# Rows of the spectral remap written four partitions apart instead of next to each other

## The chip, the cores and the metric

The kernel runs on one core of one Trainium2 chip. The metric is the device time of one execution in microseconds (us). A core has five engines that run side by side and wait for each other through semaphores: TensorE (PE; its weight loads are listed apart as PEld), VectorE (DVE), ScalarE (ACT), GpSimd (POOL) and SyncE (SP). SP issues nearly all of this kernel's DMAs; 16 DMA engines carry them out. SBUF, the on-chip memory, has 128 rows (partitions); PSUM takes TensorE's results.

## The reference

One input `x` of 2048 tokens by 448 channels goes through two branches, and a gate mixes them.

```python
S, D = 2048, 448
g = sigmoid((x * gate_w).sum(-1, keepdims=True))
# a: softmax attention, 16 heads of 28
q, k, v = split(x @ wqkv)                      # per head
a = merge(softmax(q @ k.T * 28 ** -0.5) @ v) @ wo
# b: a filter in the frequency domain
X = rfft2(x, axes=(tokens, channels))          # 2048 x 225, complex
b = irfft2(X * (w_r + 1j * w_i)).astype(bfloat16)
out = g * a + (1 - g) * b
```

Inputs and output are bfloat16. This text is about branch b and about what attention waits for while b is computed.

## The kernel before

**Attention is the frame.** The 16 heads are taken in four groups of four (`g`), the queries in four blocks of 512 (`c`): 16 stages of attention. In each, TensorE multiplies keys by queries into PSUM (`psA`, three heads' tiles at a time, and `psB`, two), ScalarE takes the exponential of the whole tile into a ring in SBUF (L1093, `ring<-psA`, `ring<-psB`), and TensorE multiplies the result with the values (`pvb`). A share of the exponentials is made on VectorE instead (L1051 and L1061, `y` and `pd`). At the end of a stage `normalise` turns the sums around: a DMA moves the sums out of `pvs` (`rs<-pvs`, L1192), VectorE takes the reciprocal (L1195) and splits it (`rhl`, L1196 and L1197), two DMAs bring the parts into eight rows (`r<-rhl`), and TensorE spreads them over the rows (`bg<-r,cst`), after which VectorE scales the stage's output (L1206).

**The spectral branch is background work.** `background` computes the two-dimensional transform as matrix products that fill TensorE's time between the attention's matmuls. First the channels are transformed (`X1`, one tile of 450 = 2 x 225 values per 128 tokens, 16 tiles). The 2048 tokens are then split as 2048 = 16 x 128, in two steps. `stage_a` multiplies each of the 16 tiles by a matrix of 128 points (three matmuls, `bg<-X,R`), VectorE copies the result from PSUM into one of three buffers `Y` (L1385), and a DMA remaps it into `U` (L1387): the 128 rows of `Y`, numbered 16 j + g with j from 0 to 7 and g from 0 to 15, become 8 rows of `U` with 16 pieces of 450 values each. After all 16 tiles, `U[:, g, :]` has in its 128 rows 16 tiles t times 8 values of j, and one matrix product per g with the table `CS` finishes the transform (`bg<-U,CR`). VectorE multiplies by the filter `w_r + i w_i` (L1427 to L1443) back into `X1`, and the inverse goes the same way: `stage_a` again with 16 remaps, then products with the table `RB` (L1465 to L1468, `bg<-CR,U`), then the inverse over the channels. Each remap moves 128 pieces of 900 bytes, 112.5 KB; there are 16 of them forward and 16 in the inverse. The first product that reads `U` waits for all 16.

**What sets the order.** A list scheduler (`Sched`) places every operation by due times and estimated costs while the program is built; each engine's order is then fixed, and each engine works strictly in that order. All DMAs named here stand in one queue, SP's. The scheduler counts a remap as 0.62 us of SP and 2.0 us until it has landed. Waits between engines come from the tiles that are written and read; a `Y` buffer is written again only when the remap that reads it has landed.

The line of the change is L1387. `rows_of(ap, row0, stride, count, dims)` (L37) names `count` rows from `row0` on, `stride` rows apart; `J` is 8, `NT` is 16, `F2` is 450. The tables `CS` and `RB` are made on the host in `fft_consts` and have their rows in the order of `U`'s rows.

## Time and profile before

| what | value |
|---|---|
| median of 3 runs | 441.5 us (441.43 to 446.78) |
| the profiled execution: its time | 443.47 us |
| its span, first to last instruction | 441.7 us |
| mean granted TensorE clock | 0.965 |
| instructions | 8904 |
| remaps `U<-Y` | 32 of 112.5 KB, 98.1 to 278.3 us, 0.61 us of SP each |
| attention's small DMAs | 15 `rs<-pvs` of 8 KB, 30 `r<-rhl` of 4 KB |
| all DMA packets | 25,902, 16.64 MB |

The profile is a record of one execution. Busy time says how long an engine was at work; a row of the timeline has the start and length of an instruction, the engine and line, what it writes and reads, and in brackets how long the engine had been idle before it and what ended that. The windows view gives busy time per engine for a stretch of the span, with the number of instructions, and then the granted TensorE clock (1.00 is full speed), the DMA engines' busy share and GB/s. The chain of waits goes back from the last instruction to what released it, step by step; its DMA pieces run from the issue to the landing. The digits of a row such as `PEclk` are tenths, one for each fortieth of the span.

### The profile page before, as it was taken

The page shows a single profiled execution, that of the slowest core. Times are in us where ns is not written, and L with a number is a line of the kernel's source. Part 1 is how long each engine was busy: PE and PEld are TensorE (multiplying, and loading weights), DVE is VectorE, ACT ScalarE, POOL GpSimd, SP SyncE. Part 2 cuts the span into 40 slices and gives each one's busy share as a digit, 9 for nine tenths or more (in the row PEclk, how much of TensorE's full clock was granted, in tenths as well). Part 3 has the DMA queues.
Part 4 walks back from the last instruction along what each step waited for, and adds up shares of the span by engine and source line. Part 5 has one row for each costly group of instructions (what it writes and reads, how often), then busy time and mean ns, then how long its engine had stood idle before and what let it go on. Part 6 is the DMA issues. An engine that isn't in the chain of part 4 may idle for free.

```text
span 441.7 us, 8904 instructions
## 1 busy us (share of the span) xinstructions
PE 405.2 (92%) x3498; PEld 145.1 (33%) x3498; DVE 341.8 (77%) x643; ACT 408.8 (93%) x379; POOL 35.3 (8%) x72
## 2 busy tenths in 40 slices
PE   8999999998998989998999959799999998999997
PEld 5443332232442232223433312212344332332233
DVE  6555678676679899998689756676877889799964
ACT  3999999998999999998999958868999999999992
POOL 3404001000022000000040000000003000000000
PEclk9999999999999999997999988957999999999999
DMA  8400100013413120110011442200001010010101
GB/s 228 113 1 3 28 11 1 2 45 70 87 42 58 39 59 22 43 40 4 2 39 32 54 50 44 47 2 24 11 25 38 14 49 3 12 34 10 36 22 62
DMA packets 25902, 16.64 MB, mean 38 GB/s; under 512 B 10456, under 2 KB 24580, under 8 KB 25860
## 3 DMA queue, kind: packets, MB, share of 16 engines
q1 hardware_dynamic: 25092, 15.82, 16.0%
q8 instruction: 27, 0.44, 0.4%
q10 hardware_dynamic: 768, 0.25, 0.3%
q14 instruction: 15, 0.12, 0.1%
HBM read 10.19 MB, written 1.84 MB: 27 GB/s over the span
## 4 chain that ended last, share of the span: by engine, by line
ACT 50%; PE 25%; issue 12%; DVE 7%; DMA 6%; ACTq 0%; DVEq 0%
ACT ring L1093 49%; PE bg L527 9%; PE pvb L527 6%; PE psA L527 5%; PE psB L527 4%; DMA rs<-pvs 2%; DMA U<-Y 2%; DVE y L1051 1%; DVE Y L1385 1%; DMA r<-rhl 1%; DMA U<-in_A_wqkv_dram 1%; DVE pd L1061 1%; PE bg L530 1%; ACT w L899 0%; DVE k L837 0%
## 5 line engine op out<-in xcount | busy, mean ns | idle before, releaser
L1093 ACT ACTIVATE ring<-psA 128x1536 bf16<-128x1536 f32 x177 | 287.9, 1626 | 12.2 <-PE psA L527 11.0
L1093 ACT ACTIVATE ring<-psB 128x1024 bf16<-128x1024 f32 x177 | 211.9, 1197 | 6.4 <-PE bg L527 3.4
L1051 DVE TENSOR_SCALAR y<-bg 128x512 uint16<-128x512 f32 x140 | 94.5, 685 | 34.2 <-PE bg L527 33.2
L1061 DVE TENSOR_SCALAR pd<-y 128x2048 uint16<-128x2048 uint16 x140 | 94.3, 691 | 1.1 <-PE pvb L527 0.6
L527 PEld LDWEIGHTS <-k 32*128 32x128 bf16 x1024 | 46.9, 91 | 132.3 <-issue 124.6
L527 PE MATMUL psA<-q,k 32*128 32x512 bf16 x531 | 72.3, 393 | 17.0 <-ACT ring L1093 13.8
L527 PE MATMUL pvb<-ring,vw 128*32 128x512 bf16 x884 | 83.0, 395 | 0.0
L527 PE MATMUL psB<-q,k 32*128 32x512 bf16 x353 | 72.4, 393 | 1.5 <-ACT ring L1093 1.3
L527 PE MATMUL pvb<-pd,vd 128*32 128x512 bf16 x560 | 57.6, 401 | 0.0
L527 PE MATMUL bg<-q,k 32*128 32x512 bf16 x140 | 53.0, 395 | 0.2 <-DVE y L1051 0.2
L527 PEld LDWEIGHTS <-vw 128*32 128x32 bf16 x884 | 20.3, 95 | 29.0 <-issue 25.9
L527 PEld LDWEIGHTS <-xT 128*128 128x128 bf16 x320 | 19.2, 99 | 19.2 <-issue 17.8
L904 POOL CAST vw<-w 128x16 bf16<-128x16 f32 x16 | 4.4, 283 | 259.3 <-ACT w L899 259.3
L527 PE MATMUL bg<-X,R 128*128 128x225 bf16 (+1 forms) x96 | 19.3, 301 | 5.0 <-DVE k L837 2.5
L1385 DVE CAST Y<-bg 128x450 bf16<-128x450 f32 x32 | 19.5, 621 | 3.5 <-PE bg L527 2.5
L960 POOL TENSOR_SCALAR vd<-vf 128x348 bf16<-128x348 f32 x16 | 19.8, 1236 | 14.5 <-DVE vf L949 6.3
L527 PEld LDWEIGHTS <-vd 128*32 128x32 bf16 x560 | 14.8, 95 | 15.7 <-issue 14.1
L527 PE MATMUL bg<-xT,wpq 128*128 128x512 bf16 (+1 forms) x60 | 18.8, 390 | 0.1
L527 PE MATMUL bg<-xT,wpk 128*128 128x512 bf16 (+1 forms) x60 | 17.9, 383 | 0.3 <-DVE xT L803 0.3
L527 PE MATMUL bg<-Bd,ZT 113*128 113x448 bf16 x64 | 18.0, 370 | 0.1
L527 PE MATMUL bg<-Bd,xT 128*128 128x450 bf16 x64 | 17.9, 359 | 0.1
L1355 DVE CAST X<-bg 128x450 bf16<-128x450 f32 x16 | 10.0, 623 | 9.0 <-PE bg L527 9.0
(114 smaller groups left out, 346.7 us busy)
## 6 DMA issues: line engine op xcount, KB each, us to landing
U<-Y SPq DMA_DIRECT2D x32, 112.5 KB
CR<-cRB SPq DMA_DIRECT2D x8, 256.0 KB
xtok<-in_A_x_dram SPq DMA_DIRECT2D x4, 448.0 KB
out_dram<-fin SPq DMA_DIRECT2D x14, 112.0 KB
CR<-cCS SPq DMA_DIRECT2D x8, 192.0 KB
Wg<-in_B_w_r_dram SPq DMA_DIRECT2D x8, 112.5 KB
Wg<-in_B_w_i_dram SPq DMA_DIRECT2D x8, 112.5 KB
U<-in_A_wqkv_dram SPq DMA_DIRECT2D x2, 252.0 KB
```

Source lines behind the costliest of these rows:

```text
L527: self.pin(self.nc.tensor.matmul(out, lhsT=lhsT, rhs=rhs, start=start, stop=stop, **kw))
L530: self.pin(self.nc.tensor.transpose(out=out, in_=in_, identity=self.c("ident")[0:n, 0:n]))
L904: self.pin(nc.gpsimd.tensor_copy(out=free_dims(self.vw[g][:], [[128, 4], [32, 4]], 4 * b * 128 + DH), in_=self.w[g][:, 4 * b:4 * b + 4, :]))
L960: self.pin(nc.gpsimd.tensor_scalar(out=self.vd[:, f, :, :, 0:DH + 1], in0=self.vf[:], scalar1=PHGAIN[f], scalar2=None, op0=ALU.mult))
L1051: self.pin(nc.vector.tensor_scalar(out=ys[:, s, :], in0=self.bgi(it), scalar1=127 * UNITS, scalar2=0.0, op0=ALU.add, op1=ALU.max))
L1061: self.pin(nc.vector.tensor_scalar(out=fl(pds).bitcast(U16), in0=fl(ys), scalar1=float(PHASE[f]), scalar2=0.25, op0=ALU.add, op1=ALU.mult))
L1093: self.pin(nc.scalar.activation(out=self.ring[:, u0:u0 + len(st), :], in_=slot[:, 0:len(st), :], func=ACT.Exp, scale=LN2 / UNITS))
L1355: self.pin(nc.vector.tensor_copy(out=self.X1[:, t, :], in_=self.bgi(it)[:, 0:F2]))
L1385: self.pin(nc.vector.tensor_copy(out=y[:], in_=self.bgi(it)[:, 0:F2]))
```

## The change

The 8 rows into which a remap writes are no longer next to each other. For tile t and row j the row in `U` was 8 t + j; it becomes `spread(t, j)` = 32 (t // 4) + 4 j + t % 4. So tile 0 wrote rows 0 to 7 and now writes rows 0, 4, 8, ... 28; tile 1 wrote rows 8 to 15 and now writes 1, 5, ... 29; tiles 4 to 7 fill rows 32 to 63, and so on. All 128 rows are still filled once. The rows of the tables `CS` and `RB` are permuted in the same way on the host, so that the products with `U` add up the same terms. The columns of the tables, and with them everything behind the products, stay. Each engine executes the same instructions in the same order with the same waits as before.

```diff
+def spread(t, j):
+    return 32 * (t // 4) + 4 * j + t % 4
...
-            CS[g, j::J, 0, j::J] = np.cos(th)
-            CS[g, j::J, 1, j::J] = np.sin(th)
-            CS[g, j::J, 2, j::J] = -np.sin(th)
+            rows = [spread(t, j) for t in range(NT)]
+            CS[g, rows, 0, j::J] = np.cos(th)
+            CS[g, rows, 1, j::J] = np.sin(th)
+            CS[g, rows, 2, j::J] = -np.sin(th)
...
-            RB[g2, j2::J, 0, j2:P:J] = np.cos(ps)
-            RB[g2, j2::J, 0, P + j2::J] = np.sin(ps)
...
+            rows = [spread(t, j2) for t in range(NT)]
+            RB[g2, rows, 0, j2:P:J] = np.cos(ps)
+            RB[g2, rows, 0, P + j2::J] = np.sin(ps)
...
-                d = self.dma(rows_of(self.U[:], t * J, 1, J, [[F2, NT], [1, F2]]), y[:], [e] + war, k, dur=0.62, lat=2.0)
+                d = self.dma(rows_of(self.U[:], spread(t, 0), 4, J, [[F2, NT], [1, F2]]), y[:], [e] + war, k, dur=0.62, lat=2.0)
```

More of the change, by code (lines that the diff above doesn't have):

```diff
@@ L73, in fft_consts @@
             ps = 2 * np.pi * (tt * aa / NT + tt * bh / S)
-            RB[g2, j2::J, 0, j2:P:J] = np.cos(ps)
-            RB[g2, j2::J, 0, P + j2::J] = np.sin(ps)
-            RB[g2, j2::J, 1, j2:P:J] = -np.sin(ps)
-            RB[g2, j2::J, 1, P + j2::J] = np.cos(ps)
+            rows = [spread(t, j2) for t in range(NT)]
+            RB[g2, rows, 0, j2:P:J] = np.cos(ps)
+            RB[g2, rows, 0, P + j2::J] = np.sin(ps)
+            RB[g2, rows, 1, j2:P:J] = -np.sin(ps)
+            RB[g2, rows, 1, P + j2::J] = np.cos(ps)
     c["RB"] = RB.reshape(NT // 2, 2, P, 4 * P).transpose(0, 2, 1, 3)
```

## The prediction

> **What bounds the kernel now.** I read the page first: its busy shares, clock row, chain and the DMA that the change touches.

> ```profile
> PE 405.2 (92%) x3498; PEld 145.1 (33%) x3498; DVE 341.8 (77%) x643; ACT 408.8 (93%) x379; POOL 35.3 (8%) x72
> PEclk9999999999999999997999988957999999999999
> ACT 50%; PE 25%; issue 12%; DVE 7%; DMA 6%; ACTq 0%; DVEq 0%
> U<-Y SPq DMA_DIRECT2D x32, 112.5 KB
> ```

> ScalarE's exponentials (L1093) carry half of the chain; DMA carries 6%. The span of 441.7 us cannot shrink below ScalarE's 408.8 us of work plus its head and tail, so what can be won is ScalarE's idle time. The table by stages says where that lies (PE, PEld, DVE, ACT, POOL busy, then clock, DMA share, GB/s):

> ```profile
> 104.50:146.00 41.50, 36.80 (x385) 14.51 (x378) 30.18 (x61) 39.08 (x40) 6.24 (x9) 1.00 0.34 62
> 146.00:204.00 58.00, 53.05 (x453) 16.95 (x451) 57.69 (x122) 58.00 (x54) 0.00 (x0) 1.00 0.15 39
> 204.00:212.00 8.00, 8.00 (x67) 3.12 (x66) 4.67 (x10) 6.63 (x8) 1.05 (x3) 0.58 0.03 4
> 255.00:304.00 49.00, 41.99 (x268) 10.56 (x268) 31.63 (x58) 35.80 (x31) 0.00 (x0) 0.76 0.23 37
> 304.00:430.00 126.00, 118.64 (x1109) 42.34 (x1107) 106.01 (x185) 126.00 (x117) 5.77 (x9) 1.00 0.08 22
> ```

> ScalarE idles 2.42 us in 104.5 to 146, 1.37 us in 204 to 212 and 13.20 us in 255 to 304, and not at all in the two long stages between and after. The first stretch is the forward remap (U<-Y, L1387) and the third holds the inverse remap and what follows. The chain of waits in order of time (start, length in us, what) shows which DMAs stand there:

> ```profile
> 102.62 3.99 DMA rs<-pvs
> 131.90 5.03 DMA U<-Y
> 140.14 4.03 DMA U<-Y
> 249.61 5.44 DMA rs<-pvs
> 258.48 4.46 DMA r<-rhl
> ```

> A U<-Y takes 4 to 5 us from issue to landing, and small transfers beside it also take 4 to 5.4 us. The timeline has one rs<-pvs (8 KB) without company, issued at 125.85 and read by VectorE at 127.75:

> ```profile
> 125.85 0.58 SPq L509 DMA_DIRECT2D rs<-pvs  x1
> 127.75 0.25 DVE L1195 RECIPROCAL rr<-rs 128x16 f32<-128x16 f32 x1 [0.76 <-DMA rs<-pvs]
> ```

> So a small transfer alone is 1.90 us; the ones in the chain are late by 2.1 to 3.5 us because they queue behind U<-Y. Nearly alone, the U<-Y of 140.14 takes 4.03 - 1.90 = 2.13 us more than the small one: 115,200 bytes in 2.13 us, 54 GB/s. Where do these 2.1 us go? The DMA view of the window 140.14 to 144.24 (40 slices of 0.10 us):

> ```profile
> GB/s 53 18 53 0 9 0 0 0 0 0 0 0 88 79 53 88 132 202 184 167 88 35 9 0 0 0 0 0 0 0 0 0 0 0 0 0 0 0 0 0
> ```

> The packets are taken up between slices 12 and 22, 1.2 to 2.3 us after the issue, at up to 202 GB/s. The landing comes 1.7 us after the last of them. The issue and the reading of Y are therefore not the long part; the write side drains for much longer than the packets are taken up.

> **The change part by part.** The two constant tables get their rows permuted on the host: no instruction, no byte more. The row in L1387 becomes four apart. Each engine's instructions, their order and their semaphores stay the same, the DMA still writes 8 rows of 16 pieces of 900 bytes, and SP still issues it in the time it did (a stride between rows is in rs<-pvs already, 0.58 us above). So the only thing with a price is how fast the 8 rows drain.

> The row for it is the 2.13 us above. [...]

> Bounds of the landing after the change, from rows: not below 1.90 us (the 8 KB transfer), and at the upper end 4.03 us (unchanged) or more (rival D). Between them stands the reading of Y, which stays as it is: packets are taken up until 2.3 us after the issue. How soon a landing follows the last packet when nothing drains is seen at the lone rs<-pvs (the window 125.85 to 127.85, slices of 0.05 us):

> ```profile
> GB/s 0 0 0 0 0 0 0 0 0 0 0 0 0 0 0 0 0 0 0 0 0 0 0 0 3 26 32 31 31 31 12 0 0 0 0 0 0 0 0 0
> ```

> Its last packets are in slice 30, at 1.55 us, and it is read at 1.90 us: 0.35 us. So I take 2.3 + 0.4 = 2.7 us. If one row accepted no more than twice today's rate, it would be 1.90 + 1.07 = 3.0 us. A U<-Y in a queue then costs those behind it about 1.1 us, the time in which its packets are taken up, instead of 2.1 us.

> Now each place, with what waited (timeline; the bracket is the idle time before the instruction and its releaser):

> ```profile
> 106.63 0.25 DVE L1195 RECIPROCAL rr<-rs 128x16 f32<-128x16 f32 x1 [2.25 <-DMA rs<-pvs]
> 108.83 1.02 ACT L1093 ACTIVATE ring<-psB 128x1024 bf16<-128x1024 f32 x1 [0.78 <-PE psB L527]
> 110.52 1.45 ACT L1093 ACTIVATE ring<-psA 128x1536 bf16<-128x1536 f32 x1 [0.66 <-PE psA L527]
> 137.03 0.63 DVE L1385 CAST Y<-bg 128x450 bf16<-128x450 f32 x1 [0.65 <-DMA U<-Y]
> 138.49 1.45 ACT L1093 ACTIVATE ring<-psA 128x1536 bf16<-128x1536 f32 x1 [0.42 <-PE psA L527]
> 144.22 0.36 PE L527 MATMUL bg<-U,CR 128*128 128x450 bf16 x1 [0.97 <-DMA U<-Y]
> 145.01 1.02 ACT L1093 ACTIVATE ring<-psB 128x1024 bf16<-128x1024 f32 x1 [0.55 <-PE bg L527]
> 248.20 1.31 SPq L509 DMA_DIRECT2D U<-Y  x2
> 255.08 0.25 DVE L1195 RECIPROCAL rr<-rs 128x16 f32<-128x16 f32 x1 [3.44 <-DMA rs<-pvs]
> 257.55 1.02 ACT L1093 ACTIVATE ring<-psB 128x1024 bf16<-128x1024 f32 x1 [1.70 <-PE psB L527]
> 258.91 1.45 ACT L1093 ACTIVATE ring<-psA 128x1536 bf16<-128x1536 f32 x1 [0.34 <-PE psA L527]
> 263.07 0.58 PE L527 MATMUL bg<-r,cst 8*128 8x512 bf16 x1 [2.76 <-DMA r<-rhl]
> 264.18 1.45 ACT L1093 ACTIVATE ring<-psA 128x1536 bf16<-128x1536 f32 x1 [2.91 <-PE psA L527]
> 278.31 0.63 SPq L509 DMA_DIRECT2D U<-Y  x1
> 284.44 0.62 PE L527 MATMUL bg<-CR,U 128*113 128x256 bf16 x4 [1.95 <-DMA rs<-pvs]
> 285.70 1.45 ACT L1093 ACTIVATE ring<-psA 128x1536 bf16<-128x1536 f32 x1 [1.73 <-PE psA L527]
> ```

> (1) At 106.6 VectorE stands 2.25 us on rs<-pvs, TensorE on VectorE, ScalarE on TensorE for 0.78 + 0.66 us. One U<-Y is ahead of that rs<-pvs; with it 1 to 2 us shorter VectorE's wait is nearly gone: 1.44 us won on ScalarE. (2) At 137.0 a Y buffer is written again only when its transfer of 131.90 has landed; at 2.7 us that is 134.6, before VectorE comes: 0.42 us. (3) At 144.2 the last forward transfer holds TensorE 0.97 us; landing 1.3 us earlier, it doesn't: 0.55 us. (4) At 255.1 rs<-pvs waits behind two U<-Y. It landed 3.5 us later than one alone; about 2 x 1 us of that goes, and since the two ahead no longer pile up (two in 1.31 us, so 0.7 us apart), up to 3 us. VectorE's 3.44 us fall to about 0.5 us and ScalarE wins 1.70 + 0.34 = 2.04 us. (5) At 263.1 r<-rhl behind a U<-Y holds TensorE 2.76 us: landing in 2.2 us instead of 4.46 leaves some 0.4 us, and ScalarE wins 2.5 of 2.91 us. (6) At 284.4 the first inverse matmul on U waits 1.95 us. The row names rs<-pvs, but that was issued 1 us before and takes 1.90; the matmul reads U, so it is the last U<-Y, issued at 278.31 behind another and out for some 6 us. At 3 us it lands at 281.3, before TensorE is free at 284.44 - 1.95 = 282.49: 1.73 us. Sum: 1.44 + 0.42 + 0.55 + 2.04 + 2.5 + 1.73 = 8.7 us.

> That leaves ScalarE's other idle time in 255 to 304: 13.20 - (2.04 + 2.91 + 1.73) = 6.5 us. It lies under a halved TensorE clock (windows; the clock is the third number from the end):

> ```profile
> 104.92:108.33 3.41, 2.11 (x23) 0.70 (x19) 1.59 (x5) 3.13 (x4) 0.25 (x1) 1.00 0.75 121
> 258.52:261.94 3.42, 1.79 (x10) 0.40 (x6) 2.08 (x4) 2.42 (x3) 0.00 (x0) 1.00 0.48 72
> 261.94:268.77 6.83, 5.70 (x34) 1.17 (x34) 2.34 (x4) 3.82 (x3) 0.00 (x0) 0.50 0.47 57
> 282.42:285.83 3.41, 1.46 (x12) 0.69 (x10) 1.64 (x4) 1.68 (x3) 0.00 (x0) 1.00 0.07 6
> 285.83:302.90 17.07, 17.07 (x95) 3.31 (x97) 10.52 (x21) 11.73 (x10) 0.00 (x0) 0.50 0.07 17
> ```

> Each halved stretch follows 3.4 us in which TensorE was busy for only 1.79 (52%) or 1.46 us (43%), and those are exactly the windows that hold waits (5) and (6). The window at 104.92, 62% busy, was followed by no halving. Without the waits the two windows fill to the 91 to 94% of the long stages, so I expect both stretches to go, and with them about 6.4 us. The halving at 204 to 212 (1.37 us) is in a stretch with hardly any DMA (share 0.03) and stays. For what becomes late next (TensorE has 94% in the stage 304 to 430, VectorE 99% in 146 to 204) I keep back 1.5 us. Gain: 8.7 + 6.4 - 1.5 = 13.6 us. The profiled execution took 443.5 us (441.7 us span and 1.8 us around it); 443.5 - 13.6 = 429.9 us. That execution is 2.0 us above the median of the runs, 441.5 us, so the forecast is 441.5 - 13.6, rounded to 428 us.

> **Rivals.** (A) The forecast, 428 us, with its own range from 424 (all of ScalarE's idle time in the three stages gone: 441.5 - 2.42 - 1.37 - 13.20 = 424.5) to 432 (half of the 6.4 us stays, and 1 us more of the waits).

> (B) The waits go, but the clock still halves near the remap. For it: the halved stretch at 204 needs no DMA, and single runs of the kernel lie 5.3 us apart (441.43, 446.78), just what ScalarE loses in the long stretch (17.07 - 11.73 us). Against it: the two stretches follow windows emptier than the one at 104.92. Then 441.5 - 8.7 + 1 = 434 us. [...]

> (C) The change doesn't do what it says: it doesn't matter which rows lie together; the drain is limited by the 8 rows themselves, or by the engines that write them, and stays 2.1 us. Rows: each row takes 14,400 B in 2.13 us, 6.8 GB/s, and no row here shows a single row taking more in a long transfer. Against it: packets are taken up at up to 202 GB/s, so the engines can read that fast. Nothing else changes: 441.5 us. [...]

> (D) Slower: consecutive transfers get into each other's way. Today each U<-Y fills the 8 rows next to those of the one before; afterwards four in a row interleave in the same 32 rows, and so share what those rows share. If two drains could overlap today and can't then, each transfer that queues behind a U<-Y is a drain later, 2.1 us at the four places (1), (4), (5) and (6): 441.5 + 8.4 = 450 us. It decides if the drain stays at 2.1 us and today's transfers do overlap. Against it: the rs<-pvs of 249.61, behind two U<-Y issued 0.7 us apart, is 3.54 us late, and two drains end to end minus these 0.7 us are 2 x 2.13 - 0.7 = 3.56 us. There is no overlap to lose.

> **How the numbers follow.** A 0.60, B 0.22, C 0.13, D 0.05. The range 424 to 438 us holds A and B with their ends, and B with only half of the 8.7 us, which a landing of 3.0 us or more could leave. What a measurement tells from no change is about 2%, 8.8 us: faster means below 432.7 us. Nearly all of A (0.58) and a third of B (0.07) lie there: 0.65. Slower than 450.3 us: about half of D, 0.02. The rest of A, B and D, and C, is within 2%: 0.33.

> **What would show it.** A U<-Y nearly alone at 2.5 to 3.3 us in the chain (right), or still near 4 us (C). rs<-pvs and r<-rhl next to it at 2 to 2.7 us, and VectorE's waits on rs<-pvs, 2.25 and 3.44 us, below 0.7 us. ScalarE's idle time in what was 255 to 304 below 4 us, with a clock row without its 5 and 8 there; if the clock stays halved there with the waits gone, B. The forecast fails if ScalarE, once free of these waits, waits just as long for something that was hidden behind them.

## The result

The changed kernel is faster: 424.85 us in the median of four runs (423.76 to 430.27) against 441.87 us before (441.43 to 446.78); the ratio is 0.958, with a 95% interval from 0.949 to 0.967. The ratio leaves out the run of 430.27 us, which lies more than 1.5% above the fastest. On the 441.5 us that the prediction started from that is 423.0 us, 18.5 us less. Forecast were 13.5 us less, 428 us, and a range from 424 to 438: right in sign and in the places that were won, too small in size, and 1 us past the lower end of the range. The profiled execution took 423.90 us with a span of 422.1 us, 19.6 us shorter than the span before.

The page of the changed kernel, with the rows that were shown of the one before:

```profile
PE 392.4 (93%) x3498; PEld 144.7 (34%) x3498; DVE 341.4 (81%) x643; ACT 406.1 (96%) x379; POOL 35.2 (8%) x72
PEclk9999999999999999999999999999999999999999
ACT 68%; PE 15%; issue 13%; DVE 2%; DMA 1%; ACTq 0%
```

The clock row has no gap any more, DMA fell from 6% of the chain to 1%, and what is left of that belongs to the loads at the start. ScalarE's share of the chain went from 50% to 68%. The table by stages, at the places of the prediction's table (the places (4) to (6), between 255 and 285 us before, now lie 8 to 14 us earlier):

```profile
104.50:146.00 41.50, 39.80 (x409) 15.84 (x408) 33.35 (x70) 41.50 (x42) 6.25 (x9) 1.00 0.25 67
204.00:212.00 8.00, 7.14 (x80) 3.01 (x72) 6.54 (x13) 8.00 (x10) 0.39 (x2) 1.00 0.02 1
255.00:290.00 35.00, 32.96 (x280) 10.69 (x279) 28.85 (x52) 35.00 (x32) 0.00 (x0) 1.00 0.13 35
```

ScalarE is busy for the whole of each: 41.50 of 41.50, 8.00 of 8.00, 35.00 of 35.00. The instructions that waited at the places (1), (3), (4), (5) and (6), in the timeline:

```profile
104.76 0.25 DVE L1201 RECIPROCAL rr<-rs 128x16 f32<-128x16 f32 x1 [0.25 <-DMA rs<-pvs]
141.06 0.36 PE L533 MATMUL bg<-U,CR 128*128 128x450 bf16 x1
247.29 0.25 DVE L1201 RECIPROCAL rr<-rs 128x16 f32<-128x16 f32 x1 [0.32 <-DMA rs<-pvs]
253.44 0.39 PE L533 MATMUL bg<-r,cst 8*128 8x512 bf16 x1
270.89 0.54 PE L533 MATMUL bg<-CR,U 128*113 128x256 bf16 x3
```

VectorE's 2.25 and 3.44 us became 0.25 and 0.32 us. TensorE's 0.97, 2.76 and 1.95 us are gone, and no copy into `Y` waits for a transfer any more (place 2). (The line numbers shown are 6 higher than before.)

### The profile page after: what moved, and what is told of

Its sections match the earlier page's. It is cut to its first block, busy times and chain, and to the rows that moved or that the text cites. A ratio compares the mean times of both kernels' runs of the same rounds, so it can differ in the third digit from the quotient of the medians.

```text
span 422.1 us, 8904 instructions
## 1 busy us (share of the span) xinstructions
PE 392.4 (93%) x3498; PEld 144.7 (34%) x3498; DVE 341.4 (81%) x643; ACT 406.1 (96%) x379; POOL 35.2 (8%) x72
## 4 chain that ended last, share of the span: by engine, by line
ACT 68%; PE 15%; issue 13%; DVE 2%; DMA 1%; ACTq 0%
ACT ring L1099 67%; PE bg L533 6%; PE psA L533 4%; PE pvb L533 3%; PE psB L533 2%; ACT w L905 1%; DMA wv<-in_A_wqkv_dram 1%; PE bg L536 1%; DMA cst<-ccst 1%; DVE y L1057 0%; DVE vw L947 0%; DVE k L688 0%; DVE xtok L1492 0%; DVE q L701 0%; DVE fin L1297 0%
## 5 line engine op out<-in xcount | busy, mean ns | idle before, releaser
L1099 ACT ACTIVATE ring<-psA 128x1536 bf16<-128x1536 f32 x177 | 296.5, 1675 | 1.6 <-PE psA L533 1.6
L1099 ACT ACTIVATE ring<-psB 128x1024 bf16<-128x1024 f32 x177 | 220.7, 1247 | 0.0
L533 PEld LDWEIGHTS <-k 32*128 32x128 bf16 x1024 | 48.8, 91 | 130.8 <-issue 122.0
L533 PE MATMUL psA<-q,k 32*128 32x512 bf16 x531 | 69.7, 381 | 19.9 <-ACT ring L1099 16.1
L533 PE MATMUL pvb<-ring,vw 128*32 128x512 bf16 x884 | 80.7, 384 | 0.0
L533 PE MATMUL psB<-q,k 32*128 32x512 bf16 x353 | 70.1, 382 | 2.1 <-ACT ring L1099 1.8
L533 PE MATMUL pvb<-pd,vd 128*32 128x512 bf16 x560 | 55.2, 384 | 0.0
L533 PE MATMUL bg<-q,k 32*128 32x512 bf16 x140 | 51.1, 383 | 0.2 <-DVE y L1057 0.2
L533 PEld LDWEIGHTS <-vw 128*32 128x32 bf16 x884 | 20.1, 94 | 26.1 <-issue 22.8
L1391 DVE CAST Y<-bg 128x450 bf16<-128x450 f32 x32 | 19.6, 621 | 3.5 <-PE bg L533 3.4
## 6 DMA issues: line engine op xcount, KB each, us to landing
U<-Y SPq DMA_DIRECT2D x32, 112.5 KB
Wg<-in_B_w_r_dram SPq DMA_DIRECT2D x8, 112.5 KB
Wg<-in_B_w_i_dram SPq DMA_DIRECT2D x8, 112.5 KB
```

The costliest lines, as they stand in the source:

```text
L533: self.pin(self.nc.tensor.matmul(out, lhsT=lhsT, rhs=rhs, start=start, stop=stop, **kw))
L1099: self.pin(nc.scalar.activation(out=self.ring[:, u0:u0 + len(st), :], in_=slot[:, 0:len(st), :], func=ACT.Exp, scale=LN2 / UNITS))
L1391: self.pin(nc.vector.tensor_copy(out=y[:], in_=self.bgi(it)[:, 0:F2]))
```

## Experiments

**What the drain depends on.** A kernel of its own sends the remap's 112.5 KB into rows that lie differently, one transfer at a time. It leaves out the computation.

```diff
+    for name, stride in (("Uone", 1), ("Utwo", 2), ("Ufour", 4), ("Ueight", 8), ("Usixteen", 16), ("Utwelve", 12),
+                         ("Vone", 1), ("Vfour", 4), ("Vthirtytwo", 32)):    # U: 8 rows of 16 pieces, V: 4 rows of 32
+        nc.sync.dma_start(out=rows_of(T[name][:], 0, stride, P // n, [[F2, n], [1, F2]]), in_=y[:])
+        nc.vector.tensor_copy(out=y[:, 0:16], in_=T[name][:, 0, 0:16])
...
+    for name, stride in (("Uone", 1), ("Ufour", 4)):     # a small transfer right behind
+        move(name, 0, stride); small(); read_small(); read(name)
+    for name, stride, second in (("Uone", 1, 8), ("Ufour", 4, 1)):     # two in a row
+        move(name, 0, stride); move(name, second, stride); read(name)
```

VectorE's timeline; the bracket is its wait for the transfer. In the first nine rows, one per pattern, SP issues the transfer 0.02 to 0.03 us after the wait begins. Then come the small transfer behind a U transfer with adjacent rows and with rows four apart, and two U transfers in a row. (The first row is from the second of three rounds, the others from the first.)

```profile
106.92 0.17 DVE L54 COPY Y<-Uone 128x16 bf16<-128x16 bf16 x1 [3.91 <-DMA Uone<-Y]
57.94 0.17 DVE L54 COPY Y<-Utwo 128x16 bf16<-128x16 bf16 x1 [3.08 <-DMA Utwo<-Y]
60.77 0.17 DVE L54 COPY Y<-Ufour 128x16 bf16<-128x16 bf16 x1 [2.65 <-DMA Ufour<-Y]
63.99 0.17 DVE L54 COPY Y<-Ueight 128x16 bf16<-128x16 bf16 x1 [3.05 <-DMA Ueight<-Y]
67.23 0.17 DVE L54 COPY Y<-Usixteen 128x16 bf16<-128x16 bf16 x1 [3.06 <-DMA Usixteen<-Y]
70.07 0.17 DVE L54 COPY Y<-Utwelve 128x16 bf16<-128x16 bf16 x1 [2.67 <-DMA Utwelve<-Y]
76.41 0.17 DVE L54 COPY Y<-Vone 128x16 bf16<-128x16 bf16 x1 [6.17 <-DMA Vone<-Y]
79.85 0.17 DVE L54 COPY Y<-Vfour 128x16 bf16<-128x16 bf16 x1 [3.26 <-DMA Vfour<-Y]
84.18 0.17 DVE L54 COPY Y<-Vthirtytwo 128x16 bf16<-128x16 bf16 x1 [4.16 <-DMA Vthirtytwo<-Y]
88.46 0.18 DVE L60 COPY pvs<-rs 128x16 f32<-128x16 f32 x1 [4.11 <-DMA rs<-pvs]
91.99 0.17 DVE L60 COPY pvs<-rs 128x16 f32<-128x16 f32 x1 [3.07 <-DMA rs<-pvs]
98.51 0.17 DVE L54 COPY Y<-Uone 128x16 bf16<-128x16 bf16 x1 [6.06 <-DMA Uone<-Y]
```

All nine waits shown lie within 0.2 us of theory P, in which four neighbouring rows share one way in: four neighbouring rows need 6.17 us, eight (two ways) 3.91 us, rows 2, 8 and 16 apart (four ways) 3.05 to 3.08 us, rows 4 and 12 apart (eight ways) 2.65 and 2.67 us, and four rows 32 apart 4.16 us, which is two ways. The rounds agree within 0.1 us, but for the four rows four apart (3.3 to 3.7 us) and 32 apart (4.2 to 4.3 us). Rows 8 and 16 apart are slower (3.0 us) than rows 4 and 12 apart (2.6 us) although they are spread wider, and four rows 32 apart (4.1 us) cost as much as eight next to each other (3.9 us): nearness alone (Q) and a fixed limit per row (R) are both out as what makes the old order slow. One way for all 112.5 KB takes 6.1 us; less the 1.9 us of a small transfer alone, which was measured in the whole kernels, 4.2 us are left, by this estimate 27 GB/s. The small transfer issued some 0.7 us after a U transfer is read 3.40 us after its own issue behind adjacent rows and 2.32 us behind rows four apart (alone 1.9 us): the queueing is real, and it shrinks, though the 1.5 us behind adjacent rows are less than the 2 us that P had. Two transfers in the old order end 5.9 to 6.0 us after the first issue, so they drain one after the other although their rows are in different groups; the overlap that rival D would have lost does not exist. In the new order, with both in the same ways, VectorE can read 3.7 to 3.8 us after the first issue. With eight ways the next limit shows. The trace closes each U transfer with eight packets of 4 bytes (a remap of the changed kernel, at 137.86 us, too: 128 packets of 900 bytes and eight of 4) and each V transfer with four, from which I take it that eight and four DMA engines write them, one row each. With four ways, eight rows (2 apart) need 3.1 us and four rows (4 apart) 3.3 to 3.7 us; with eight ways eight rows need 2.6 us, about 0.7 us for the 14,400 B of one row, an estimate of some 21 GB/s. Whether it is the engine or the row that takes no more, the probe can't tell.

**A third row order.** The remapped rows 16 apart, with tables to match:

```diff
 def spread(t, j):
-    return 32 * (t // 4) + 4 * j + t % 4
+    return 16 * j + t
```

> Rows 16 apart (16 j + t) in place of four apart, tables permuted to match; all else as in the changed kernel. P: four ways, a remap lands in 2.9 us instead of 2.5; VectorE's and TensorE's waits on the DMAs stay below about 1 us and the time is that of the changed kernel within 1%, 424 to 428 us. Q: 2.5 us and the same time. If any added 0.4 us of landing were exposed at the six places, 424 + 2.4 = 426 us.

425.74 us in the median (425.05 to 430.06), ratio 0.963 (0.956 to 0.970): within 1% of the changed kernel. One wait on a transfer by TensorE came back, 0.54 us on `r<-rhl`, where the changed kernel has none:

```profile
254.78 0.37 PE L533 MATMUL bg<-r,cst 8*128 8x512 bf16 x1 [0.54 <-DMA r<-rhl]
```

So most of the gain is there once a remap lands in 3.0 us instead of 3.9 (the probe's figures for rows 16 and 1 apart); the last 0.4 us of the landing, down to the 2.6 us of rows four apart, are worth little.

**One half of the change at a time.** Forward remaps alone:

```diff
-                d = self.dma(rows_of(self.U[:], spread(t, 0), 4, J, ...
+                d = self.dma(rows_of(self.U[:], spread(t, 0) if inv == 0 else t * J, 4 if inv == 0 else 1, J, ...
```

> Forward remaps write rows four apart, the 16 inverse remaps neighbouring rows as before (the table CS permuted, RB not). Theory T: ScalarE's idle time comes from the waits, place by place, and the halved clock behind 255 us from the waits there. Then the 2.4 us of 104 to 146 are won and nothing of the 13 us after 255: 438 to 440 us, with VectorE waiting 3 us on rs<-pvs and TensorE 2 to 3 us on r<-rhl and U, and one or two halved stretches right behind them. Rival H: the halving is chance and independent of the waits; then halved stretches are as likely elsewhere, and the time lies between 432 and 440 us from run to run.

439.36 us in the median (433.43 to 442.68), ratio 0.984 (0.974 to 0.995), which rests on the runs of 433.43 and 438.59 us. The waits after 250 us are those of the kernel before, one of them shorter (1.49 us for 2.76):

```profile
252.44 0.25 DVE L1201 RECIPROCAL rr<-rs 128x16 f32<-128x16 f32 x1 [3.37 <-DMA rs<-pvs]
260.47 0.40 PE L533 MATMUL bg<-r,cst 8*128 8x512 bf16 x1 [1.49 <-DMA r<-rhl]
283.45 0.62 PE L533 MATMUL bg<-CR,U 128*113 128x256 bf16 x4 [1.95 <-DMA rs<-pvs]
```

The clock was halved from 253.9 to 257.3, from 260.7 to 270.9 and from 284.6 to 294.8 us, behind each of the three, and once more from 199.2 to 206.1. The spread of the run times would nearly suit H as well; that the stretches stand where T has them is what speaks for T.

The inverse remaps alone, by the same edit with the two cases exchanged:

> The other half alone: forward remaps write neighbouring rows as before, the inverse ones rows four apart. T: the 2.4 us of 104 to 146 stay lost, the 13 us after 255 are won with about 2 us of slower restarts: 426 to 428 us, no halved stretch behind 255 us. Together the two halves' gains, about 3 and 14 us, should add up to the 17 us of the whole change. H: a halved stretch in this kernel as often as in the one before.

431.22 us (430.02 to 433.15), ratio 0.974 (0.968 to 0.980). The place, the waits and the clock after 255 us came as T had it:

```profile
255.00:290.00 35.00, 32.59 (x268) 10.70 (x268) 28.99 (x55) 35.00 (x32) 0.00 (x0) 1.00 0.18 45
```

ScalarE is busy throughout, at the full clock. But the time is 3 to 5 us above the expectation, because the clock was halved at two places which have no transfer wait, 159.6 to 166.4 and 204.0 to 210.8 us, and all four runs had 10 to 21 us of halved clock. There H has a point. By the ratios the two halves gain 1.6% and 2.6%, together the whole change's 4.2%, but the first has an interval from 0.5 to 2.6%. By the medians they gain 3.7 and 11.9 us, together 15.6 us against 17.0 us for the whole change: about additive, no closer than that.

**Is it the empty TensorE that halves the clock?** The kernel before, with matmuls of zeros at the waits (5) and (6):

```diff
+            if n == 8:
+                for _ in range(22):
+                    self.mm(self.bgi(it)[:, 0:256], self.zero[:, 0:P], self.zero[:], True, True)
             self.mm(self.bgi(it), self.c("sel8", 8), r8[:], True, True)
...
+                        if g == 0 and fb == 0 and ri == 0:
+                            for _ in range(15):
+                                self.mm(self.bgi(it)[:, 0:256], self.zero[:, 0:P], self.zero[:], True, True)
```

> The kernel before, with neighbouring rows, and 22 matmuls of zeros (256 columns, 0.107 us each, 2.4 us) just ahead of the spread of the sums in stage 8, at the wait (5), and 15 (1.6 us) just ahead of the first inverse product, at the wait (6). They run while TensorE would stand there; their result is overwritten. No transfer is any faster. Theory T: an emptier TensorE in those 3.4 us is what halves the clock; the waits of VectorE and ScalarE stay, the halved stretches behind 262 and 286 us go, and with them 5 to 6 us: 436 to 438 us, with 7 to 10 us of halved clock instead of 27 to 41. Rival H: the halving comes from something else there (the phase of the run, or the total load): as many halved us as before, 441 to 446 us, plus up to 1 us for fillers that are late.

437.54 us (433.78 to 439.36) against 442.99 us, ratio 0.986 (0.977 to 0.996). At (6) the fillers occupy the wait, ScalarE still idles 1.40 us at the next exponential (1.73 before), as its timeline shows:

```profile
284.70 1.81 PE L527 MATMUL bg<-zero 128*128 128x256 bf16 x15
287.65 1.45 ACT L1093 ACTIVATE ring<-psA 128x1536 bf16<-128x1536 f32 x1 [1.40 <-PE psA L527]
```

The table by stages of the same run has the clock (the 1.00 before the last two columns) whole behind it:

```profile
286.38:303.00 16.62, 15.84 (x137) 5.02 (x135) 14.84 (x28) 15.35 (x14) 0.00 (x0) 1.00 0.08 19
```

With no transfer faster, 3.5 to 20.1 us of halved clock remained per run; 7 to 10 us were expected. In the kernel before, on the same chip, it was 17.5 to 41.0 us (one run, whose record says 121 us at an ordinary time, is left out). At (5) a halved stretch stayed, from 258.3 to 265.1 us, right behind wait (4), which had no fillers; those for (5) ran only from 264.6 us on, so they test nothing. At (6) the transfers and ScalarE's wait stayed and only TensorE's emptiness went, and the halving went with it. That rests on one profile with fillers against two without (before, forward alone), and on the halved time of four runs, whose highest (20.1 us) lies above the lowest before (17.5 us).

**Halved time against time.** Each run's halved time follows from its mean clock and span, as (1 - clock) x 2 x span:

| kernel | us of halved clock: time of the run in us |
|---|---|
| before (five of twenty) | 17.5: 438.96; 27.2: 440.70; 30.8: 442.11; 34.5: 444.72; 41.0: 447.66 |
| changed | 0: 423.76; 0: 423.90; 6.8: 425.80; 20.6: 430.27 |
| forward alone | 10.4: 433.43; 23.6: 438.59; 30.7: 440.13; 37.9: 442.68 |
| inverse alone | 11.1: 430.02; 10.3: 431.20; 13.7: 431.25; 20.7: 433.15 |

Within each kernel a halved us goes with about 0.3 us more (0.33 for a straight line through all twenty runs of the kernel before, 0.31 for the changed one). It is most of what the runs of one kernel differ by, not all: seven more of the runs before had 27 us of it, and they lie between 440.07 and 443.18 us. Carried to no halving at all, beyond any run, that line puts the kernel before at about 433 us, some 9 us above the changed one; by this estimate these 9 us are waits. The other 7 to 8 us are halved time, some 30 us less some 7 of it at 0.3.

**Is ScalarE now the only bound?** ScalarE has no wait above 0.2 us from 11 to 411 us in the changed kernel, so work was taken from it: one more tile of keys (then two) on VectorE.

```diff
-    ND = [0, 1, 2, 2, 2, 3, 2, 3, 2, 1, 3, 2, 3, 3, 3, 3]
+    ND = [0, 1, 2, 2, 2, 3, 2, 3, 2, 2, 3, 2, 3, 3, 3, 3]
```

> The changed kernel with one more tile of keys in stage 9 made on VectorE instead of ScalarE (ND[9] from 1 to 2). ScalarE was without a wait from 11 to 411 us, so its work is the bound: four units of 512 fewer are 2.24 us / 5 x 4 = 1.8 us less. VectorE gets 4 x 0.69 + 4 x 0.69 = 5.5 us more and was 82% busy in 255 to 290. If ScalarE alone is the bound: 422.1 us in runs without halving. If VectorE or TensorE, 93 to 94% busy, is next, it is no better than 424 us.

> As the run with one more tile on VectorE, and another in stage 11 (ND[11] from 2 to 3). If ScalarE alone is the bound: 3.6 us less than the changed kernel, 420.3 us. If the engines behind it are: VectorE's or TensorE's work then ends waits of ScalarE in 255 to 330, and it is 424 us or more.

430.84 and 430.87 us, ratios 0.975 (0.968 to 0.981) and 0.974 (0.965 to 0.983): 6 us slower than the changed kernel. Two of the runs with one more tile had no halved clock at all and took 430.3 and 430.5 us. The order of the whole kernel was planned anew, and ScalarE then waits for the products with the values (`pvb`) and at the end, 8.7 us there (`t` and `fin`) where the changed kernel has 5.0. With one more tile:

```profile
ACT t L1295 <- PE psB L533: 5.4, 1, 5.4
ACT ring L1099 <- PE pvb L533: 3.9, 3, 2.4
ACT fin L1295 <- PE bg L533: 3.3, 1, 3.3
```

So less work for ScalarE alone wins nothing here. TensorE ends these waits; whether its load or the new order makes it late is not told apart.

**More fillers.** The changed kernel, with a higher floor for TensorE's busy share in the planner:

```diff
-HAMW, HAMF = 3.4, 0.734
+HAMW, HAMF = 3.4, 0.78
```

> The changed kernel with the planner's floor for TensorE's busy share (HAMF) at 0.78 in place of 0.734: 114 zero matmuls instead of 51, placed by the planner in its idle time; the rest of the order shifts with them. Runs of the changed kernel lie between 423.8 us without halved clock and 430.3 us with 20.6 us of it. If emptier windows halve the clock there too: no run above 426 us, halved time under 7 us. If the fillers get in the way of the score matmuls, ScalarE waits for TensorE again and even runs without halving are above 424 us.

> As ham078 with the floor at 0.82 and 143 zero matmuls. Same reading: with halving gone all runs within 1 us of 423.8 us; with fillers in the way, slower than that in every run.

With 0.78, 431.99 us (431.76 to 433.06); with 0.82, 429.06 us (428.91 to 429.26); ratios 0.976 (0.968 to 0.984) and 0.969 (0.963 to 0.976). With 0.82 the runs have 0 to 0.9 us of halved clock, and all four lie within 0.35 us, which fits a spread that comes from the clock. But the fillers and the order that goes with them cost 5 us, as the second of the two expected readings had it, and no version here beats the changed kernel.

## Why the prediction was right or wrong

**The drain (right, on an assumption).** From the lone small transfer, the packets' times and the landing it concluded that the write side is slow, and it took 2.7 us for a landing: packets until 2.3 us and the 0.4 us that follow the last one when nothing drains. That rows four apart leave nothing to drain was the author's assumption, and the 8.7 us for the waits rest on it; no run shows it. The runs showed in its place a landing of 2.53 us in the changed kernel and of 2.6 us in the probe, where 2.6 - 1.9 = 0.7 us are left for the drain, against 4.2 us by one way and 2.0 us by two; which limit sets these 0.7 us, of the engines or of the rows, is open. What makes the old order slow, the nine patterns show: some 27 GB/s per way by the probe's estimate, and four rows 32 apart that land like eight neighbours (4.1 and 3.9 us).

**The waits (1) to (6) (right in place).** Each was to be nearly gone, and is; the half changes show that each half's waits are its own transfers'. The sum of 8.7 us was 0.4 us too low, see below.

**The clock (right for the two stretches).** Both go with the waits; the fillers at (6) speak for the emptiness as the cause there. In each of the ten profiles of whole kernels the clock changes only at steps of 3.41 us (the halved stretches of the kernel before, 6.83 and 17.07 us, are two and five of them), and where these steps lie differs from profile to profile. All six of these windows in which TensorE was under 55% busy (30 to 52%, the kernel's start and end aside) were followed by a halved one. So it also matters how a wait falls on the windows: wait (4) left one 57% busy at 255.1 us in the kernel before, and no halving followed; in the run with zero matmuls it left one 40% busy at 254.8 us, and halving followed. Emptiness is not all, though. None of the four windows between 57 and 62% was followed by halving, but thirteen between 64 and 83% were, and many others of that fullness were not. Eleven of the thirteen begin at 152 to 160 or 196 to 201 us; what decides there is open.

**What failed: the size of the sum, and the floor under it.** The step that set the range was that the span "cannot shrink below ScalarE's 408.8 us of work" and that only its idle time can be won: that work itself fell, to 406.1 us. Four terms of the sum were mis-sized. First, "I keep back 1.5 us" for what becomes late next: nothing became late, ScalarE's idle time between the first and the last exponential went from 17.2 to 0.2 us. Second, "The halving at 204 to 212 (1.37 us) ... stays": it did not occur in the profiled run. That is partly luck: in six of the ten profiles, with slow remaps or without, a halved stretch begins between 199 and 204 us, and two runs of the changed kernel have 6.8 and 20.6 us of halved time at places that no profile shows. Third, 0.4 us were to remain at (5); none did. Fourth, a term that was missing, and the one that lies below the floor: a stalled exponential costs more than the idle time. Between the first and the last exponential, ScalarE's time outside of idle gaps is, with the number of gaps over 0.06 us in it:

| kernel | before | forward alone | inverse alone | rows 16 apart | changed |
|---|---|---|---|---|---|
| gaps | 24 | 18 | 11 | 5 | 1 |
| us outside of gaps | 403.8 | 403.5 | 402.6 | 401.6 | 401.2 |

That is about (403.8 - 401.2) / 23 = 0.12 us for each restart, 2.7 us in all. The pace of the exponentials agrees: one of `psA` that starts after a gap takes 1.45 us, but in an unbroken run of the changed kernel the next one starts 1.35 us (median) after it. The groups of the page show it too, first of the kernel before, then of the changed one (busy, mean ns of one, idle before):

```profile
L1093 ACT ACTIVATE ring<-psA 128x1536 bf16<-128x1536 f32 x177 | 287.9, 1626 | 12.2 <-PE psA L527 11.0
```

```profile
L1099 ACT ACTIVATE ring<-psA 128x1536 bf16<-128x1536 f32 x177 | 296.5, 1675 | 1.6 <-PE psA L533 1.6
```

One exponential is recorded longer after the change (1675 ns against 1626), and 352 of the 354 start inside the one before instead of 327, so the records overlap more; ScalarE's union of busy time, in which an overlap counts once, still fell from 408.8 to 406.1 us. Idle time and restarts make 17.0 + 2.7 = 19.7 us, and the spans differ by 19.6 us; likewise the forecast 13.6 us and the four terms, 1.5, 1.37, 0.4 and 2.7 us, make 19.6 us.

**The rivals.** B fails at its two stretches: with the inverse remaps spread, no profile has a halved stretch after 241 us, the kernel's end aside. It is half right in a way that it did not say, since some halved time comes and goes with the run at places without a wait. C falls with the probe: with eight rows and eight closing packets in either case, the landing goes from 3.9 to 2.6 us. D falls with the two transfers in a row, as its own counter-argument had it. The range was too narrow below: its lower end took all of ScalarE's idle time as the most that could be won.

## What to carry to other kernels

Where a transfer lands in few rows, compare its landing with the time in which its packets are taken up: if the landing is far behind (here 4.03 us against 2.3 us), the rows' ways in can be the limit, and rows chosen to use more of them cost no instruction here (8904 before and after), since a host table could absorb the permutation. The price of such a transfer was here mostly paid by the small ones behind it and by whoever waits for those in order. Add to a wait's length the restart of the waiting engine (0.12 us of ScalarE here) and, for TensorE, what a half-empty 3.4 us can do to its clock afterwards: the six windows under 55% here were each followed by halving, at about 0.3 us per halved us.

## What the runs showed of the hardware that was not expected

Two transfers from one queue into different groups of eight neighbouring rows did not overlap in the probe: they ended 5.9 to 6.0 us after the first issue, where one alone took 3.9 us. The halved clock explains most of the difference between runs of one kernel, at about 0.3 us per halved us, and it was nearly gone in the kernel with 143 zero matmuls (0 to 0.9 us left). An exponential of ScalarE that started after a gap cost about 0.12 us beyond the gap (2.6 us over 23 gaps).
